# Reordering the opening of a one-core Trainium2 kernel: where decays are clipped, when they are stored, and how the first gates arrive

## The chip, the core and the metric

The kernel runs on one core of a Trainium2 chip. The core has five engines, each with its own stream of instructions: TensorE (PE: matrix products, written to PSUM), VectorE (DVE), ScalarE (ACT), GpSimd (POOL) and SyncE (SP, which here only issues transfers, or DMAs, between DRAM and on-chip memory). ScalarE and GpSimd issue a few transfers too. An engine takes its instructions in order, and one that waits for a semaphore holds everything behind it. The metric is the device time of one execution, in microseconds (us), as the median of several runs. Less is better.

## What is computed

Two blocks in a row. The first is a state-space recurrence (Mamba-2 style) over 4 sequences of 768 tokens with 8 heads of width 32 and state size 16; the second mixes 4 experts, each a two-layer network of width 1024, over the resulting 3072 tokens of width 256.

```python
log_a = np.log(np.clip(a, 1e-06, 1.0))
for c in range(nc):
    ...
    cum = np.cumsum(la, axis=-1)
    L = np.exp(cum[:, :, :, None] - cum[:, :, None, :]) * causal
    CB = np.einsum('bhin,bhjn->bhij', Cc, Bc)
    y_intra = np.einsum('bhij,bhjd->bhid', CB * L, xc)
    y_inter = np.einsum('bhin,bhnd->bhid', Cc, state) * decay_to_i[:, :, :, None]
    y[:, :, sl] = y_intra + y_inter
    state = decay_full[:, :, None, None] * state + np.sum(Bx, axis=2)
...
p = domain_probs / (domain_probs.sum(-1, keepdims=True) + 1e-09)
for e in range(E):
    h = np.maximum(x @ w1[e], 0.0)
    out += p[:, e:e + 1] * (h @ w2[e])
```

The decays `a` are clipped to [1e-6, 1]; running products of them weigh the scores C·B; the weighted scores times x are the outputs y. The probabilities p, one for each token and expert, are the gates of the second block.

## The kernel before

Tokens are cut into 24 chunks of 128; four chunks, one of each sequence, make a block of 512 tokens, so there are 6 blocks. The two-layer networks run over a block in 8 steps (expert by half of its width), 48 steps in all; steps n = 2 to 47 form a loop, and each uses a scheme with seven products instead of eight, whose weight sums GpSimd makes once (`sum_w1`, `sum_w2`) and stores for later blocks. Recurrence work for the next block is woven into the loop. Steps 0 and 1 of the first block use plain products (`plain_first`, `plain_gated`, `plain_second`).

The order of all instructions is written out by hand: each engine's queue is the program's order, and semaphores are set from what tiles are written and read. A transfer issued by SP or ScalarE also waits until the one eight before it in the program's order has landed, since eight semaphores are used in turn.

One chunk goes through these helpers:

- `clip_first(engine, c)`, for chunks 0 to 2 only: clips the raw decays, already laid out for the products, into a_q (two operations at L279 and a small memset at L287).
- `spread(c, homes)`: 16 passes at L362 copy the decays over partitions into PSUM (tiles named a).
- `decays(c)`: VectorE's scans at L395 make the running products LT; GpSimd's L400 makes the part of MT that feeds the state. From chunk 3 on the scans read a tile ab that `load_decays` (L147, SP's queue) brings from the DRAM copy acut_d.
- `masks(c)`: two ScalarE operations (L411) that prepare B.
- `scores(cs, homes)`: TensorE's L429, tile g.
- `masked(cs, rs)`: VectorE's L441 multiplies g by LT into MT. `aside(c, 3)` does one of the four head groups by ScalarE (copy, L447) and GpSimd (L448).
- `outputs(cs, homes)`: TensorE's L488 gives y; ScalarE copies it to yT (L501) and the state part to A (L508, L509, L511).

The decays of all chunks are clipped and cut into a_cut by GpSimd (L302 to L307) and stored by ScalarE's queue with `store_decays` (L314 to acut_d, L311 to ac_d). The gates pr are normalized by GpSimd and VectorE (L294 to L300), turned round by TensorE (L323, tile pp), copied (L326) and stored to p_d (L327, SP's queue). Each later expert's gates come back from p_d with `load_gate` (L347), spread over all partitions. Those of the first block's first expert are made without that transfer: `spread_gate` spreads them by four products with columns of the identity (L337, tile gp), and `keep_gate` copies the result (L343).

`turn(n, w)` (L776) issues n products of width w x 128 whose result nobody reads. In what follows they are called unread products. They multiply the tile `ones`, which VectorE sets at L230.

The opening, in order (main part):

```python
turn(1); turn(1, 2); spread(0, banks); turn(1, 3)
masks(0); scores([0], homes); turn(1, 2)
decays(0); aside(0, 3); store_decays(0)
masks(1); spread(1, banks); masked([0], (2, 0, 1)); clip_first(nc.gpsimd, 2)
load_rows(2); load_w1(1); store_decays(1)
turn_gates(ps_att, "att"); turn(1, 2); outputs([0], ATT)
scores([1], ...); decays(1); aside(1, 3)
load_x(2); load_rows(3); load_decays(3); load_w2(0); load_x(3)
spread(2, ...); spread_gate((0, 1), ps_att, "att"); masked([1], (0, 1, 2)); masks(2)
outputs([1], ...); spread_gate((2, 3)); keep_gate(); sum_w1(0, 0)
load_w2(1); load_w1(2); load_w2(2); decays(2); plain_first(0, 1, (0,)); ...
```

Of the kernel before, what the change touches and what calls it, by code (L numbers as in the profile page):

```python
# [8 lines left out]
FP32 = mybir.dt.float32  # L9
# [3 lines left out]
P = 128  # L13
# [4 lines left out]
def kernel(  # L18
# [40 lines left out]
    nc = tc.nc  # L59

    NCH, _, W = xbc.shape
    E, DM, F = w1.shape
# [4 lines left out]
    CPB = BLK // P  # L67
    NBLK = NCH // CPB
    T = NCH * P
# [8 lines left out]
    def real(c):  # L78

        return c % CPB * NBLK + c // CPB  # L80
# [7 lines left out]
    att = ctx.enter_context(tc.tile_pool(name="att", bufs=2))  # L88
    ffn = ctx.enter_context(tc.tile_pool(name="ffn", bufs=2))
    ps_att = ctx.enter_context(tc.tile_pool(name="ps_att", bufs=2, space=bass.MemoryType.PSUM))  # L90
    ps_f = ctx.enter_context(tc.tile_pool(name="ps_f", bufs=1, space=bass.MemoryType.PSUM))
    ps_s = ctx.enter_context(tc.tile_pool(name="ps_s", bufs=1, space=bass.MemoryType.PSUM))
# [5 lines left out]
    p_d = tc.dram_tile([T // P, E, P], FP32, name="p_d")  # L98
# [7 lines left out]
    HALF = P // 2  # L106
# [5 lines left out]
    def turned_round(c):  # L112


        return c >= CPB and c % 2 == 1

    def load_rows(c):

        xb = load.tile([P, OCT + P], FP32, tag="xb", name="xb", bufs=4)
        src = xbc[real(c)][:, WX:]  # L120
        if turned_round(c):
            nc.sync.dma_start(out=xb[:HALF, OBT:], in_=src[HALF:])
            nc.sync.dma_start(out=xb[HALF:, OBT:], in_=src[:HALF])
        else:
            nc.sync.dma_start(out=xb[:, OBT:], in_=src)
        st.setdefault(c, {})["xb"] = xb
# [17 lines left out]
    def load_decays(c):  # L144
        ab = load.tile([P, NQ, TRI], FP32, tag="ab", name="ab")
        for t in range(NT):
            nc.sync.dma_start(  # L147
                out=ab[HALF * t:HALF * t + HALF].rearrange("p q s -> p (q s)"),
                in_=acut_d[t, real(c)].rearrange("q s -> (q s)").partition_broadcast(HALF))
        st.setdefault(c, {})["ab"] = ab  # L150
# [73 lines left out]
    a_sb = const.tile([NCH * NH // 2, 2, P], FP32, name="a_sb")  # L224
# [4 lines left out]
    ones = const.tile([P, P], FP32, name="ones")  # L229
# [3 lines left out]
    for queue, c in ((nc.sync, slice(0, 1)), (nc.scalar, slice(1, SPREAD))):  # L233
        queue.dma_start(
            out=a_raw.rearrange("(q r) c t s -> q r c (t s)", q=NQ)[:, 0, c],
            in_=a.rearrange("(i k) (q t) s -> k q i (t s)", k=NBLK, t=NT)[0][:, c])
# [4 lines left out]
        out=a_sb, in_=a.rearrange("c h s -> (c h) s").rearrange("(p r) s -> p r s", r=2))  # L241
# [6 lines left out]
    ident = const.tile([P, P], FP32, name="ident")  # L248
# [19 lines left out]
    for q in range(NQ):  # L268
        rows = slice(32 * q, 32 * q + 32)
# [8 lines left out]
    def clip(engine, v, top=1.0, out=None):  # L278
        engine.tensor_scalar(out=v if out is None else out, in0=v, scalar1=1e-6, scalar2=top,  # L279
                             op0=ALU.max, op1=ALU.min)  # L280

    def clip_first(engine, c):


        clip(engine, a_raw[:, c], own, a_q[:, c, :, :P])
        clip(engine, a_raw[:, c, :, HALF:], own, a_q[:, c, :, P:])
        engine.memset(a_q[:, c, :, 0:P + 1:P], 0.0)  # L287

    clip_first(nc.vector, 0)
    clip_first(nc.vector, 1)  # L290


    pairs = const.tile([P, T // P, 2], FP32, name="pairs")
# [5 lines left out]
    nc.vector.reciprocal(total_p, total_p)  # L299
    nc.gpsimd.tensor_mul(pr, pr, total_p.to_broadcast([P, T // P, E]))  # L300

    clip(nc.gpsimd, a_sb)  # L302

    a_cut = const.tile([NCH * NQ, NT, TRI], FP32, name="a_cut")
    nc.gpsimd.tensor_copy(a_cut[:, :, :P], a_sb)
    nc.gpsimd.tensor_copy(a_cut[:, :, P:], a_sb[:, :, HALF:])
    nc.gpsimd.memset(a_cut[:, :, 0:P + 1:P], 0.0)  # L307

    def store_decays(kind):
        if kind:  # L310
            nc.scalar.dma_start(  # L311
                out=ac_d.rearrange("c h s -> (c h) s").rearrange("(p r) s -> p r s", r=2), in_=a_sb)
        else:
            nc.scalar.dma_start(  # L314
                out=acut_d.rearrange("t c q s -> (c q) t s"), in_=a_cut)

    gate = {}

    def turn_gates(pool, tag):

        rows = T // P * E
        pp = pool.tile([rows, P], FP32, tag=tag, name="pp")
        nc.tensor.transpose(pp, pr.rearrange("p i e -> p (i e)"), ident)  # L323
        p_sb = const.tile([rows, P], FP32, name="p_sb")
        gate["rows"] = p_sb
        nc.scalar.copy(out=p_sb, in_=pp)  # L326
        nc.sync.dma_start(out=p_d.rearrange("i e s -> (i e) s"), in_=p_sb)  # L327

    def spread_gate(parts, pool=None, tag=None):

        p_sb = gate["rows"]
        if 0 in parts:
            gate["all"] = pool.tile([P, CPB, P], FP32, tag=tag, name="gp")
        g = gate["all"]
        for i in parts:
            r = real(i) * E
            nc.tensor.matmul(  # L337
                out=g[:, i], lhsT=ident[:T // P * E, r:r + 1].to_broadcast([T // P * E, P]),
                rhs=p_sb, start=(i == 0), stop=True, skip_group_check=True)

    def keep_gate():
        gate[0, 0] = ffn.tile([P, CPB, P], FP32, tag="gate", name="gate", bufs=3)
        nc.scalar.copy(out=gate[0, 0], in_=gate["all"])  # L343

    def load_gate(k, e):
        g = gate[k, e] = ffn.tile([P, CPB, P], FP32, tag="gate", name="gate", bufs=3)
        nc.sync.dma_start(out=g, in_=p_d.rearrange(  # L347
            "(i k) e s -> k e i s", k=NBLK)[k, e].partition_broadcast(P))
# [4 lines left out]
    def spread(c, homes):  # L353


        s = st[c]
        s["a"] = []
        for q, (pool, tag) in enumerate(homes):
            k = slice(32 * q, 32 * q + 32)
            b = pool.tile([P, TRI], FP32, tag=tag, name="a")  # L360
            for t in range(NT):
                nc.tensor.matmul(  # L362
                    out=b[HALF * t:HALF * t + HALF], lhsT=ones[k, :HALF], rhs=a_q[k, c, t],
                    start=True, stop=True, tile_position=(32 * q, HALF * t), skip_group_check=True)
            s["a"].append(b)
# [39 lines left out]
    def masks(c):  # L405


        s = st[c]
        m = s["btm"] = att.tile([HN, 2, NT, HALF], FP32, tag="btm", name="btm")
        for t in range(NT):  # L410
            nc.scalar.mul(  # L411
                m[:, :, t], s["xb"][:, OBT:OBT + P].rearrange("p (h j) -> p h j", h=2),
                tmask[:, t:t + 1])

    def scores(cs, homes):

        for c in cs:
            st[c]["g"] = {}
        for r, (pool, tag) in enumerate(homes):
            g = pool.tile([P, len(cs), 3, HALF], FP32, tag=tag, name="g")  # L420
            for j, c in enumerate(cs):
                st[c]["g"][r ^ 2 * turned_round(c)] = g[:, j]
        for j, c in enumerate(cs):
            s = st[c]
            for h in range(2):
                for r in range(NQ):
                    k = slice(32 * r, 32 * r + 32)
                    g = s["g"][r ^ 2 * turned_round(c)].rearrange("p h i -> p (h i)")
                    nc.tensor.matmul(  # L429
                        out=g[:, P * h:P + HALF * h],  # L430
                        lhsT=s["btm"][k, h].rearrange("p t j -> p (t j)"),
                        rhs=s["xb"][k, OCT + HALF * h:OCT + P],
                        start=(j == 0 and h == 0), stop=True, tile_position=(32 * r, 0),
                        skip_group_check=True)
# [334 lines left out]
    ATT = ((ps_att, "att"), (ps_att, "att"))  # L769
    banks = ((ps_f, "X"), (ps_f, "Y"), (ps_s, "acc2"), (ps_s, "acc3"))  # L770

    def turn(n, w=4):

        for _ in range(n):
            t = ps_att.tile([P, w, P], FP32, tag="att", name="t")
            nc.tensor.matmul(out=t, lhsT=ones, rhs=ones.unsqueeze(1).to_broadcast([P, w, P]),  # L776
                             start=True, stop=True)

    turn(1)
    turn(1, 2)  # L780
    spread(0, banks)
    turn(1, 3)
    masks(0)
    scores([0], homes)
    turn(1, 2)
    decays(0)
    aside(0, 3)
    store_decays(0)
    masks(1)
    spread(1, banks)  # L790
    masked([0], (2, 0, 1))
    clip_first(nc.gpsimd, 2)
    load_rows(2)
    load_w1(1)
    store_decays(1)
    turn_gates(ps_att, "att")
    turn(1, 2)
    outputs([0], ATT)
    scores([1], ((ps_s, "acc0"), (ps_s, "acc1"), (ps_att, "att"), (ps_f, "X")))
    decays(1)  # L800
    aside(1, 3)
    load_x(2)
    load_rows(3)
    load_decays(3)
    load_w2(0)
    load_x(3)
    spread(2, ((ps_s, "acc2"), (ps_s, "acc3"), (ps_f, "Y"), (ps_s, "acc0")))
    spread_gate((0, 1), ps_att, "att")
    masked([1], (0, 1, 2))
    masks(2)  # L810
    outputs([1], (ATT[0], (ps_s, "acc1")))
    spread_gate((2, 3))
    keep_gate()
    sum_w1(0, 0)
    load_w2(1)
    load_w1(2)
# [53 lines left out]
    for n in range(PLAIN, NS):  # L870
        k, r = divmod(n, SPB)
# [8 lines left out]
        e = r // JJ  # L880
# [138 lines left out]
```

## Time and profile before

| | |
|---|---|
| median of 9 runs | 642.23 us (639.24 to 645.97) |
| profiled execution: its time | 642.23 us |
| profiled execution: span from first to last instruction | 640.4 us |
| TensorE busy | 634.4 us, 99% |
| VectorE busy | 470.4 us, 73% |
| ScalarE busy | 124.0 us, 19% |
| GpSimd busy | 109.0 us, 17% |
| transfers | 122.16 MB, mean 191 GB/s |

The profile is of one execution. Its page gives busy times, the chain of work that ended last (followed back from the last instruction), and groups of instructions with what ended the idle time before them. A timeline lists instructions in order of time: start, length, engine and line, output and inputs, how many. The line numbers are those of the kernel before. "Landing" of a transfer is the time from its issue to its last completion.

Because the share of TensorE is 99%, the page as a whole says little of the change, which lies in the first 27 us or so. GpSimd, at 17% of the span, is busy for most of the first 60 us: its work is nearly all in the opening.

### The profile page before, as it was taken

Reading aid. Unit: us, or ns where it says so; the run is one execution under the profiler, and the core shown is the slowest. Engines: PE = TensorE matmul, PEld = TensorE weight load, DVE = VectorE, ACT = ScalarE, POOL = GpSimd, SP = SyncE. Lnnn points to the kernel's source line nnn. Section 1 sums busy time; section 2 is a strip of 40 time slices with the busy share of each in tenths; the row PEclk is TensorE's granted clock in tenths of the full one; section 3 lists DMA queues with packets and bytes.
Section 4 is the critical chain, followed back from the end, with each engine's and each line's share of the span. In section 5 each row is a group of like instructions: output and inputs, shape, how many; then the busy total and the mean of one; then the engine's idle time right before and its main releaser. Section 6 shows DMA issues by size and latency. Waiting matters only on the chain.

```text
span 640.4 us, 10765 instructions
## 1 busy us (share of the span) xinstructions
PE 634.4 (99%) x4089; PEld 545.0 (85%) x4089; DVE 470.4 (73%) x814; ACT 124.0 (19%) x314; POOL 109.0 (17%) x169
## 2 busy tenths in 40 slices
PE   8999999999999999999999999999999999999997
PEld 4888888888888888888888888888888888888886
DVE  6667989787776878777778768678876676756555
ACT  3211121212121221122121212122111212111110
POOL 6785738020000002000002000000200000100001
PEclk9999999999999999999999999999999999999999
DMA  6899788397646468546729754647786754157001
GB/s 195 238 338 336 230 212 339 115 262 224 204 118 198 181 196 270 171 161 195 249 79 291 252 169 118 208 169 207 246 206 204 253 175 133 60 142 248 3 1 34
DMA packets 104136, 122.16 MB, mean 191 GB/s; under 512 B 30440, under 2 KB 89108, under 8 KB 104084
## 3 DMA queue, kind: packets, MB, share of 16 engines
q1 hardware_dynamic: 101032, 111.60, 56.9%
q0 software_dynamic: 2432, 9.50, 3.8%
q8 instruction: 32, 0.52, 0.3%
q10 hardware_dynamic: 620, 0.37, 0.2%
q14 instruction: 20, 0.16, 0.1%
HBM read 108.56 MB, written 12.88 MB: 190 GB/s over the span
## 4 chain that ended last, share of the span: by engine, by line
PE 99%; DVE 1%; issue 0%; ACT 0%
PE acc L654 44%; PE X L569 25%; PE Y L569 19%; PE acc L635 2%; PE g L429 2%; PE y L488 2%; PE X L618 1%; PE Y L618 1%; PE y L466 1%; PE t L776 1%; PE a L362 0%; PE gp L337 0%; DVE qmask L270 0%; DVE a_q L279 0%; PE turned L701 0%
## 5 line engine op out<-in xcount | busy, mean ns | idle before, releaser
L581 DVE TENSOR_TENSOR z<-Y,snap 128x512 f32<-128x512 f32 x138 | 94.9, 688 | 137.8 <-PE Y L569 69.3
L654 PE MATMUL acc<-hT,wt 128*128 128x256 f32 x736 | 181.0, 379 | 0.0
L576 ACT COPY snap<-X 128x512 f32<-128x512 f32 x138 | 80.8, 586 | 425.1 <-PE X L569 423.1
L654 PEld LDWEIGHTS acc<-hT,wt 128*128 128x128 f32 x736 | 139.8, 190 | 19.0
L654 PE MATMUL acc<-h,wt 128*128 128x256 f32 x552 | 143.6, 383 | 0.0
L569 PE MATMUL X<-yS,wt 128*128 128x256 f32 x552 | 141.7, 379 | 0.0
L569 PEld LDWEIGHTS X<-yS,wt 128*128 128x128 f32 x552 | 104.8, 190 | 14.5 <-issue 0.3
L654 PEld LDWEIGHTS acc<-h,wt 128*128 128x128 f32 x552 | 103.1, 190 | 15.0
L591 DVE SCALAR_TENSOR_TENSOR h<-z,gate 128x512 f32<-128x512 f32 x138 | 99.2, 719 | 3.5 <-PE acc L635 0.4
L569 PE MATMUL Y<-yT,wt 128*128 128x256 f32 x368 | 94.4, 379 | 0.0
L569 PEld LDWEIGHTS Y<-yT,wt 128*128 128x128 f32 x368 | 68.8, 190 | 10.6
L598 DVE TENSOR_TENSOR hT<-h,hT 128x512 f32<-128x512 f32 x92 | 66.5, 723 | 1.8
L598 DVE TENSOR_TENSOR hT<-h,h 128x512 f32<-128x512 f32 x92 | 62.2, 717 | 1.1
L569 PE MATMUL X<-yT,wt 128*128 128x256 f32 x184 | 47.3, 379 | 0.0
L569 PE MATMUL Y<-yS,wt 128*128 128x256 f32 x184 | 47.2, 379 | 0.0
L400 POOL TENSOR_TENSOR MT<-xb,LT 128x128 f32<-128x128 f32 x20 | 9.5, 473 | 187.7 <-PE Y L569 98.3
L395 DVE TENSOR_TENSOR_SCAN LT<-ab,own_i 128x384 f32<-128x384 f32 x42 | 40.8, 982 | 0.0
L591 DVE SCALAR_TENSOR_TENSOR h<-X,gate 128x512 f32<-128x512 f32 x50 | 34.5, 689 | 8.5 <-PE X L569 4.5
L569 PEld LDWEIGHTS X<-yT,wt 128*128 128x128 f32 x184 | 34.9, 190 | 4.9 <-issue 0.2
L569 PEld LDWEIGHTS Y<-yS,wt 128*128 128x128 f32 x184 | 35.0, 190 | 4.7
L381 POOL TENSOR_TENSOR cts<-xb,dec 128x128 f32<-128x128 f32 x20 | 8.9, 465 | 156.0 <-DVE dec L378 91.1
L441 DVE TENSOR_TENSOR MT<-g,LT 128x192 f32<-128x192 f32 x94 | 26.0, 348 | 2.2 <-PE g L429 2.2
(103 smaller groups left out, 345.4 us busy)
## 6 DMA issues: line engine op xcount, KB each, us to landing
wt<-in_w_dram SPq DMA_DIRECT2D x112, 256.0 KB, 6.1
wt<-w_d SPq DMA_DIRECT2D x40, 640.0 KB, 7.1
wt<-w_d SPq DMA_DIRECT2D x40, 512.0 KB, 8.3
ab<-acut_d SPq DMA_DIRECT2D x42, 192.0 KB, 3.2
gate<-p_d SPq DMA_DIRECT2D x23, 256.0 KB, 6.7
w_d<-wt POOLq DMA_DIRECT2D x8, 640.0 KB, 6.4
wt<-in_w_dram SPq DMA_DIRECT2D x40, 128.0 KB, 9.0
xb<-in_xbc_dram SPq DMA_DIRECT2D x38, 128.0 KB, 3.1
```

Source lines behind the costliest of these rows:

```text
L395: nc.vector.tensor_tensor_scan(out=LT[:, i * w:i * w + w], data0=s["a"][i], data1=own_i.rearrange("p q h i -> p (q h i)")[:, :w], initial=0.0,
L429: nc.tensor.matmul(out=g[:, P * h:P + HALF * h], lhsT=s["btm"][k, h].rearrange("p t j -> p (t j)"), rhs=s["xb"][k, OCT + HALF * h:OCT + P] ...
L441: nc.vector.tensor_mul(s["MT"][:, q, :, :HALF], s["g"][q], s["LT"][:, q])
L488: nc.tensor.matmul(out=y, lhsT=halves(c)[rows, h, OX[t] + 32 * q:OX[t] + 32 * q + 32], rhs=m, start=(k == 0 and h == 0), stop=(h == 1), ti ...
L569: nc.tensor.matmul(out=f[bank][:, j], lhsT=wt1[n][:, w, j * P:j * P + P], rhs=rhs, start=(i in (1, 2, 5) and j == 0), stop=(j == JJ - 1), ...
L576: nc.scalar.copy(out=s, in_=first[n]["X"])
L581: nc.vector.tensor_add(z, first[n]["Y"], first[n][i])
L591: nc.vector.scalar_tensor_tensor(out=h, in0=first[n][src], scalar=0.0, in1=g.unsqueeze(1).to_broadcast([P, JJ, HB]), op0=ALU.max, op1=ALU. ...
L598: nc.vector.tensor_sub(h[o], h[x], h[y])
L618: nc.tensor.matmul(out=f[bank][:, j], lhsT=wt1[n][:, w, j * P:j * P + P], rhs=yT[k][:, i, cols], start=(i == 0 and j == 0), stop=(i == 1), ...
L635: nc.tensor.matmul(out=acc[k, u][:, half], lhsT=w2_op(n, w)[:, j], rhs=hid[n][f"{i + 1}{b}"][:, j], start=(begins and i == 0 and j == 0), ...
L654: nc.tensor.matmul(out=acc[k, u][:, half], lhsT=w2_op(n, w)[:, j], rhs=rhs[:, j], start=(begins and j == 0), stop=(n % SPB == SPB - 1 and ...
```

## The change

It does the following:

- Chunk 1's `clip_first` moves from VectorE to GpSimd, after the gates' normalization.
- The clip and cut of all decays (`cut_decays`) move in GpSimd's order from before chunk 0's state part to after chunk 2's `clip_first`.
- Both `store_decays` and `load_decays(3)` move to after the outputs of chunk 1. In ScalarE's queue the stores thus stand behind chunk 1's copies, and in SP's queue the load of chunk 3's decays stands behind `load_w2(0)` and `load_x(3)`.
- `turn_gates` moves up to before the scores of chunk 0, and its store to p_d goes out on ScalarE's queue instead of SP's.
- `spread_gate` and `keep_gate` are gone; `load_gate(0, 0)` brings the first expert's gates from p_d, on SP's queue behind `load_w1(1)`.
- The unread products multiply a constant of the program (1.0, one column, repeated) which is set before the engines are released. There are two of width 512 and one of width 256, instead of one of 512, one of 384 and three of 256.
- Chunk 1's outputs use the same PSUM tag for both halves.

```diff
     clip_first(nc.vector, 0)
-    clip_first(nc.vector, 1)
...
-    clip(nc.gpsimd, a_sb)
+    clip_first(nc.gpsimd, 1)
...
-    nc.gpsimd.tensor_copy(a_cut[:, :, :P], a_sb)
-    nc.gpsimd.tensor_copy(a_cut[:, :, P:], a_sb[:, :, HALF:])
-    nc.gpsimd.memset(a_cut[:, :, 0:P + 1:P], 0.0)
+    def cut_decays():
+        clip(nc.gpsimd, a_sb)
+        nc.gpsimd.tensor_copy(a_cut[:, :, :P], a_sb)
+        nc.gpsimd.tensor_copy(a_cut[:, :, P:], a_sb[:, :, HALF:])
+        nc.gpsimd.memset(a_cut[:, :, 0:P + 1:P], 0.0)
...
-        gate["rows"] = p_sb
         nc.scalar.copy(out=p_sb, in_=pp)
-        nc.sync.dma_start(out=p_d.rearrange("i e s -> (i e) s"), in_=p_sb)
+        nc.scalar.dma_start(out=p_d.rearrange("i e s -> (i e) s"), in_=p_sb)
...
-            nc.tensor.matmul(out=t, lhsT=ones, rhs=ones.unsqueeze(1).to_broadcast([P, w, P]),
-                             start=True, stop=True)
-    turn(1)
+            one = nc.const_aps.tensor(1.0, [P, 1])
+            nc.tensor.matmul(
+                out=t, lhsT=one.to_broadcast([P, P]),
+                rhs=one.unsqueeze(1).to_broadcast([P, w, P]), start=True, stop=True)
+    turn(2)
+    spread(0, banks)
+    masks(0)
+    turn_gates(ps_att, "att")
     turn(1, 2)
-    spread(0, banks)
-    turn(1, 3)
-    masks(0)
     scores([0], homes)
-    turn(1, 2)
     decays(0)
     aside(0, 3)
-    store_decays(0)
     masks(1)
     spread(1, banks)
     masked([0], (2, 0, 1))
     clip_first(nc.gpsimd, 2)
+    cut_decays()
     load_rows(2)
     load_w1(1)
-    store_decays(1)
-    turn_gates(ps_att, "att")
-    turn(1, 2)
+    load_gate(0, 0)
     outputs([0], ATT)
     scores([1], ((ps_s, "acc0"), (ps_s, "acc1"), (ps_att, "att"), (ps_f, "X")))
     decays(1)
     aside(1, 3)
     load_x(2)
     load_rows(3)
-    load_decays(3)
     load_w2(0)
     load_x(3)
     spread(2, ((ps_s, "acc2"), (ps_s, "acc3"), (ps_f, "Y"), (ps_s, "acc0")))
-    spread_gate((0, 1), ps_att, "att")
     masked([1], (0, 1, 2))
     masks(2)
-    outputs([1], (ATT[0], (ps_s, "acc1")))
-    spread_gate((2, 3))
-    keep_gate()
+    outputs([1], ATT)
+    store_decays(0)
+    store_decays(1)
+    load_decays(3)
     sum_w1(0, 0)
```

## The prediction

> **What bounds the kernel now.** I read the shares of the chain that ended last first, then that chain in order of time, then each engine's timeline over the first 30 us. The page's shares:
>
> ```profile
> PE 99%; DVE 1%; issue 0%; ACT 0%
> ```
>
> TensorE is the bound. In the chain in order of time (start us, us, what) it is left only in the opening:
>
> ```profile
> 4.48 0.10 DVE a_q L279
> 4.57 0.04 issue
> 4.62 0.94 PE a L362 x16
> ...
> 8.26 0.37 DVE MT L441
> 8.62 0.04 issue
> 8.67 1.22 PE t L776 x2
> ...
> 16.22 0.64 PE gp L337 x4
> 16.86 1.73 PE X L618 x8
> ...
> 26.57 0.54 PE y L488 x32
> 27.11 3.65 PE acc L635 x16
> ```
>
> See three things. TensorE's first needed products (decays of chunk 0, tile a) wait for VectorE's clip at 4.57. From 8.67 on TensorE has one gap over 0.1 us (0.18 at 22.27) until the last transposes. So a microsecond is won or lost only by what precedes the long stretch of weight products. The checkpoint I use is the end of chunk 3's outputs, y(3), at 27.11: behind it both kernels issue the same products. The timelines of the opening (start us, us busy, engine, line; the bracket is idle time and what ended it):
>
> ```profile
> 5.88 1.07 POOL L279 TENSOR_SCALAR a_sb<-a_sb 96x256 f32<-96x256 f32 x1
> 7.70 0.10 POOL L307 MEMSET a_cut<- 96x4 f32 x1
> 8.41 0.36 ACTq L314 DMA_DIRECT2D acut_d<-a_cut  x1
> 8.74 0.59 POOL L448 TENSOR_TENSOR MT<-gs,LT 128x192 f32<-128x192 f32 x1 [0.50 <-ACT gs L447]
> 9.45 1.93 POOL L279 TENSOR_SCALAR a_q<-a_raw,own 128x256 f32<-128x256 f32 x2
> 11.43 0.11 POOL L287 MEMSET a_q<- 128x4 f32 x1
> 11.93 1.10 PE L488 MATMUL y<-MT,xb 64*32 64x144 f32 x32
> 13.87 1.12 SPq L147 DMA_DIRECT2D ab<-acut_d  x2
> 15.61 0.61 PE L488 MATMUL y<-MT,xb 64*32 64x144 f32 x32
> 21.77 1.80 DVE L395 TENSOR_TENSOR_SCAN LT<-ab,own_i 128x384 f32<-128x384 f32 x2
> 23.48 1.13 DVE L441 TENSOR_TENSOR MT<-g,LT 128x192 f32<-128x192 f32 x4
> ```
>
> The same 32 output products take 1.10 at 11.93 and 0.61 at 15.61: TensorE runs at half its later rate until about 13, though the profile's granted clock reads 1.00 in every slice. And chunk 3's decays leave (acut_d) at 8.41, come back (ab) from 13.87, and are scanned only at 21.77, with time to spare.
>
> **The change, step by step.**
>
> **1. Start.** The unread products no longer wait for VectorE's ones (0.84 to 1.00), so they start near 0.74, when the engines are released, not 1.06. Four passes of 512 columns at the record spacings of before (1.02 for the first, 0.85 for the next) end at 0.74 + 1.02 + 3 x 0.85 = 4.3. Tile a(0) still waits for VectorE at 4.57. Worth nothing; its cover is that clip.
>
> **2. VectorE loses chunk 1's clip** (0.39 net). The reciprocal moves from 5.06 to about 4.57, so GpSimd's pr (0.35) ends at 5.30 instead of 5.79 and the transpose pp can follow a(0) at 5.5. Between a(0) and the scores, 384 columns of unread product become pp plus 256: pp 0.25, product 0.9, scores from 6.65 (7.07 before), done 7.8 (8.23). VectorE's scans still end at 7.47. Gain 0.4.
>
> **3. Two unread products of 256 columns go**, with pp from its old place. At 8.67 to 9.82 and 10.69 to 11.93 they cost 1.15 + 1.24. Chunk 1's a now follows the scores at 7.8, if GpSimd has its clip by then: GpSimd takes it at 5.38, for 1.93 + 0.16 by the row of 9.45, done 7.47. It is hidden, by 0.3. Then a(1) ends at 8.67, and y(0) waits for GpSimd's product of head group 3 (scores out by ScalarE 7.93 to 8.25, then 0.59): 8.92. y(0) thus starts 3.0 us earlier than 11.93.
>
> **4. GpSimd becomes the wait.** Behind that product stand chunk 2's clip (2.10: 9.03 to 11.13), all decays' clip and cut (5.88 to 7.80 before, 1.93: done 13.1), and only then chunk 1's state part (0.41) and head group 3 (0.59): done 14.2, against 15.25 before. VectorE's share of chunk 1 is ready at 12.0. So y(1) stalls 2.2 us on TensorE and ends at 14.8, against 16.24. This returns 1.6 of the 3.0 us. If chunk 2's clip slowed beside VectorE, each 0.1 is 0.1 here; the a_sb clip ran beside VectorE's scans at its usual pace, so I add nothing.
>
> **5. The gate's products go** (two at 0.64 by the chain) and ScalarE's 0.59 copy. The second 0.64 hid ScalarE's yT copies, so 0.3 appears: X starts at 15.15, against 16.86: 1.7 earlier. In their place the gates go out on ScalarE's queue at about 7.3 and come back as one 256 KB transfer on SP's queue. The store of before took 2.8 us from issue to landing (trace: 11.46 to 14.24), acut_d took 4.3 on ScalarE's queue: back-load issued at 10.2 to 11.7. Its 512 packets of 34 ns (trace, at 29 to 35 us) are 1.1 us of 16 engines, behind weights that landed at 13.8: landed by 15 to 16. The next gate took 6.2 from issue, which would be 16.4 to 17.9. VectorE asks for it at X's end, 16.9, with the masked scores of chunk 2 queued behind; they have 1 us of slack. Bounds 0 to nothing visible, since step 6 waits longer anyway. Value 0.
>
> **6. The decays' round trip moves behind y(1).** ScalarE issues acut_d only after y(1)'s copies, near 15.2 (6.8 later than 8.41; at worst 16.0 behind the four state copies, which end 1.15 after the first). Landing takes 2.8 (p_d's row) to 4.3 (acut_d's own); I take 3.7, since the queue is loaded but less than then: 18.9. SP, which now has the ab loads behind x(3), waits there. Two issues, then landing 3.2 after the second (the page's median for ab) to 4.4 (trace: 14.39 to 18.82); I take 3.8 as the queue has run nearly empty: 18.9 + 0.65 + 3.8 = 23.35. Then by the rows of 21.77 and 23.48 scan and masked scores take 2.84, and y(3) ends 0.55 after: 26.7. Without this wait y(3) would end at 15.15 + 10.25 (its distance from X before) = 25.4. So 1.3 of the 1.7 us is given back. Ends: 18.0 + 0.65 + 3.2 + 3.4 = 25.3, no wait at all; 20.3 + 0.65 + 4.4 + 3.4 = 28.75.
>
> **7. Behind SP's wait** stand the transfers of w2(1), w1(2), w2(2), chunk 4 and the next gate: about 3 us later (w2(1) 21.3, was 18.24). GpSimd's sums of w2 start 25.7 instead of 24.07. First uses: TensorE takes w1(2) at 40.96, its sums at 44.4 (GpSimd had them at 32.0), the gate at 43.7 (landed 35.3). At least 8 us of cover: 0. If it were gone, at most those 3 us.
>
> **Sum.** y(3) ends at 26.7 instead of 27.11: -0.4. Profiled span 640.4 becomes 640.0; the profiled execution took 642.23, which is also the median, so 1.8 lies around the span: **641.8 us**.
>
> [...]
>
> **Rivals.**
>
> *A, the opening's gain survives.* The round trip is short: acut_d as fast as p_d, ab at the median. For it: the stores no longer compete with the first weights. Then y(3) ends at 25.3 to 25.5, and if TensorE also reaches full rate before y(0) (0.49 less there), 24.9: -1.7 to -2.2, 640.0 to 640.5. Against it: both ends must be the short ones.
>
> *B, slower: TensorE stays at half rate.* Before, it reached full rate 4.4 us after its last gap (8.67 to 13.1). The changed order leaves gaps at 8.7 and 10.0 (0.2 to 0.3 each) and 2.2 us at 12.0; the stretch without gaps begins at about 15.2. If every gap counts as much as the one before 8.67 did, full rate comes 4.4 us after that, near 19.6; y(1) is 0.5 later (1.10 against 0.61), X starts at 15.65, and the 3.95 us until 19.6 do only 2.0 us of work: y(3) ends at 25.4 + 0.5 + 2.0 = 27.9, +0.8, 643.0; with twice that time to full rate another 2.2 is lost, 645.2. It decides over step 6 as soon as the half rate lasts past 18. Against it: from 0.74 to 8.67 TensorE has only one gap of 0.3, so it may be warm by 8.
>
> *C, slower: the round trip at its loaded end* (4.3 and 4.4, ScalarE's issue at 16.0): y(3) ends at 28.75, +1.6: 643.9. Each microsecond beyond a landing of 23.8 costs one.
>
> *D, GpSimd's clip is not hidden in step 3*: a(1) late by what it exceeds; absorbed by step 4, so no change from the forecast.
>
> **Chances.** Forecast 0.45 (with D), A 0.20, B 0.20, C 0.12, something else 0.03. About 0.5%, 3.2 us, is what a measurement of this kernel can tell from no change (the nine runs spread from 639.24 to 645.97). No case reaches it by itself; the scatter of a median, about 1 us, and a mis-sized term do. Faster by over 0.5% (under 639.0): a third of A, some of the rest, 0.10. Slower (over 645.4): a quarter of B, a third of C, the rest: 0.13. Within: 0.77. The range reaches from A less 1 us to the late end of B: 639.0 to 645.0.
>
> **What would show it.** y(0) near 8.9 and y(1) cut in two by a wait on GpSimd's MT L448; X near 15.2; ScalarE's store of acut_d near 15.2 and VectorE's scan of ab near 23.4 with TensorE idle before y(3) by 1 to 1.5 us. The first y group at 0.6 instead of 1.1 means the clock came early; X at over 3 us for its 8 passes means B. I am wrong if the scan starts before 22 (A) or after 25 (C), if VectorE waits for the gate at 17 to 19, or if gaps appear on TensorE after 30 us.

## The result, and the profile after

| | before | after |
|---|---|---|
| median | 642.27 us (54 runs, 639.24 to 646.29) | 647.95 us (17 runs, 644.5 to 650.14) |
| ratio to before | | 1.0082, 95% interval 1.0063 to 1.0101 |
| profiled execution | 642.23 us, span 640.4 | 645.14 us, span 643.4 |

The change costs 5.7 us, where 0.4 less was forecast. The range ended at 645.0. The profiled execution of after took 2.8 us less than the median; a second profile, at the median, is shown further down.

The shares of the chain that ended last, after:

```profile
PE 95%; DMA 2%; SPq 1%; POOL 1%; issue 0%; DVE 0%; ACT 0%; POOLq 0%
```

TensorE no longer has 99%: transfers, their issues and GpSimd hold 4 of the points. The chain in order of time (start us, us, what) says where:

```profile
7.45 3.44 DMA xb<-in_xbc_dram
...
15.05 6.39 DMA acut_d<-a_cut
21.45 0.02 issue
...
24.90 3.62 DMA wt<-in_w_dram
28.52 0.02 issue
28.54 1.29 PE y L474 x25
29.83 3.65 PE acc L621 x16
```

The checkpoint, the end of y(3), is at 29.83 against 27.11. From there on after stays 2.72 us behind before: the first products and their results h are the same 2.7 us late at 38 us, at 64 us and at 540 us. So the loss is made before 30 us. The long step is the store of the decays, 6.39 us. (The chain names the weights `wt` last. They landed at 28.52; by the timeline what y(3) reads was ready at 28.48, so at most 0.04 us of its wait is theirs.) The timeline of after (start us, us busy, engine, line; in brackets the idle time before it and what ended it):

```profile
7.27 0.35 ACTq L329 DMA_DIRECT2D p_d<-p_sb  x1
8.23 1.16 PE L474 MATMUL y<-MT,xb 64*32 64x144 f32 x32 [0.18 <-DVE MT L427]
10.91 1.06 POOL L279 TENSOR_SCALAR a_sb<-a_sb 96x256 f32<-96x256 f32 x1
11.43 0.39 SPq L333 DMA_DIRECT2D gate<-p_d  x1
13.31 1.62 PE L474 MATMUL y<-MT,xb 64*32 64x144 f32 x32 [1.84 <-POOL MT L386]
15.05 0.33 ACTq L317 DMA_DIRECT2D acut_d<-a_cut  x1
15.16 3.78 PE L604 MATMUL X<-yT,wt 128*128 128x256 f32 x8 [0.23 <-ACT yT L487]
18.98 0.69 DVE L577 SCALAR_TENSOR_TENSOR h<-X,gate 128x512 f32<-128x512 f32 x1 [5.54 <-PE X L604]
21.51 1.12 SPq L147 DMA_DIRECT2D ab<-acut_d  x2
26.13 1.81 DVE L381 TENSOR_TENSOR_SCAN LT<-ab,own_i 128x384 f32<-128x384 f32 x2 [3.65 <-DMA ab<-acut_d]
28.07 0.41 POOL L386 TENSOR_TENSOR MT<-xb,LT 128x128 f32<-128x128 f32 x1 [5.50 <-DMA wt<-in_w_dram]
28.54 1.29 PE L474 MATMUL y<-MT,xb 64*32 64x144 f32 x32 [1.34 <-DMA wt<-in_w_dram]
```

Read it from the end. y(3) starts 0.06 us after GpSimd's state part (28.07 + 0.41), which follows VectorE's scan (26.13 + 1.81 = 27.94), which waited 3.65 us for the decays to come back. SP could ask for them only at 21.51, when the store had landed.

Two things are new. The stretch from 12 to 20 us, with the busy time of each engine, the mean granted clock, the share of the transfer engines and GB/s at the end of a line:

```profile
12.00:16.00 4.00, 2.46 (x34) 1.72 (x35) 1.44 (x4) 1.57 (x8) 3.73 (x8) 0.58 0.50 93
16.00:20.00 4.00, 4.00 (x24) 2.84 (x24) 0.84 (x2) 0.01 (x1) 0.22 (x2) 0.56 1.02 236
```

First, the transfers move 93 GB/s from 12 to 16 us (before: 250): the gates' transfer is running then. Second, the granted clock is 0.58 and 0.56. The records behind these means give full rate from 5.85 us, half from 12.68, full again from 19.51. That is why X takes 3.78 instead of 1.89 us.

### The profile page after: what moved, and what is told of

Its sections match the earlier page's. It is cut to its first block, busy times and chain, and to the rows that moved or that the text cites. A ratio compares the mean times of both kernels' runs of the same rounds, so it can differ in the third digit from the quotient of the medians.

```text
span 643.4 us, 10747 instructions
## 1 busy us (share of the span) xinstructions
PE 634.0 (99%) x4077; PEld 544.4 (85%) x4077; DVE 471.1 (73%) x811; ACT 123.4 (19%) x313; POOL 112.8 (18%) x172
## 2 busy tenths in 40 slices
DMA packets 104663, 122.41 MB, mean 190 GB/s; under 512 B 30456, under 2 KB 89636, under 8 KB 104612
## 4 chain that ended last, share of the span: by engine, by line
PE 95%; DMA 2%; SPq 1%; POOL 1%; issue 0%; DVE 0%; ACT 0%; POOLq 0%
PE acc L640 44%; PE X L555 25%; PE Y L555 19%; PE acc L621 2%; PE y L474 2%; PE g L415 2%; PE y L452 1%; DMA acut_d<-a_cut 1%; DMA wt<-in_w_dram 1%; PE Y L604 1%; PE X L604 1%; DMA xb<-in_xbc_dram 1%; SPq L136 0%; SPq L187 0%; SPq L175 0%
## 5 line engine op out<-in xcount | busy, mean ns | idle before, releaser
L584 DVE TENSOR_TENSOR hT<-h,h 128x512 f32<-128x512 f32 x92 | 64.0, 736 | 1.1
```

The costliest lines, as they stand in the source:

```text
L584: nc.vector.tensor_sub(h[o], h[x], h[y])
```

## Experiments

The loss was put to three theories. **G**: the gates' transfer takes some 7 us and holds back what is beside and behind it. **W**: TensorE's wait for GpSimd at y(1) lets the clock fall to half. **R**: the late round trip of the decays is long by itself. Each median is compared with runs of before made beside it on the same chip (their medians are 642.2 to 642.4); ratios are to these, and intervals are 95%. Edits are shown in short, without the bodies of helpers that come back.

### Undoing parts of the change

**Gates by products again**, the rest as after:

```diff
-    load_gate(0, 0)
+    spread_gate((0, 1), ps_att, "att")
...
-    outputs([1], ATT)
+    outputs([1], (ATT[0], (ps_s, "acc1")))
+    spread_gate((2, 3))
+    keep_gate()
```

> The changed kernel, but the first expert's gates are made by products as before (no gate transfer among the first loads); decays still stored late. Three theories. G (the gate transfer, 6.9 us from issue to landing, holds back the loads and stores around it): acut_d lands 3.5 to 4.3 us after its issue instead of 6.4, chunk 3's scan starts near 23.5, y(3) ends near 26.7, median 642 to 643.5. W (the wait of y(1) for GpSimd lets TensorE's clock fall to half): that wait is still there, 1.5 to 2 us, X takes about 3.5 us, median 645 to 648. R (the late round trip of the decays is long in itself): scan after 25, y(3) ends after 29, median 645 or more.

645.76 us, ratio 1.0054 (1.0030 to 1.0078). The decays' store landed in 1.9 us (19.48 to 21.42) and y(3) had no wait, as G says. But the run brought a fault of its own: with one transfer fewer, the eight semaphores fell differently, and ScalarE's store of the gates had to wait for another load. In the trace its semaphore was last used by the first load of x(1), issued at 6.14 and landed at 10.53; in after it was that of the second load of x(0), landed at 7.19. (The semaphores go round in an order that is not quite that of the source: in after the store takes its turn behind `load_w1(1)`, here behind `load_rows(3)`.) ScalarE's copy stood behind it:

```profile
10.61 0.39 ACTq L330 DMA_DIRECT2D p_d<-p_sb  x1
11.04 0.32 ACT L450 COPY gs<-g 128x192 f32<-128x192 f32 x1 [5.15 <-DMA xb<-in_xbc_dram]
```

y(0) then waited 3.6 us, and the clock fell from 10.73 to 20.97. So 645.76 is no price for the gates' transfer.

**Decays' clip, stores and load at their old places**, gates by the transfer:

```diff
+    clip_first(nc.vector, 1)
...
-    clip_first(nc.gpsimd, 1)
...
+    cut_decays(); store_decays(0)
...
+    store_decays(1)
...
+    load_decays(3)
...
-    store_decays(0); store_decays(1); load_decays(3)
```

> The changed kernel, but chunk 1's clip, the clip and cut of all decays, their stores and chunk 3's load as before; the gate still comes by a transfer. G: the loads behind the gate are still late, VectorE waits for the gate or TensorE for chunk 2's x until 18 to 19, y(3) ends near 27.5 to 28.5, median 643 to 645. W: y(1) no longer waits for GpSimd, the clock stays full, median 640 to 642. R: the scan of chunk 3 does not wait, median 640 to 642.

643.85 us, 1.0025 (1.0006 to 1.0045): 4.1 us less than after. In its profile no wait of TensorE above 0.3 us is left in the opening, yet X took 3.78 us: full rate came only at 19.92, though the unread products start as in after.

**Both undone**, only the start as after, which is the two edits above together:

```diff
+    clip_first(nc.vector, 1)
...
+    store_decays(0)
...
-    load_gate(0, 0)
+    store_decays(1)
+    load_decays(3)
+    spread_gate((0, 1), ps_att, "att")
...
+    spread_gate((2, 3))
+    keep_gate()
```

> Both undone: gates by products and decays as before; what stays of the change are the unread products from the program's constants, fewer of them, and the gates' transposition moved up. All theories: faster than before, since y(0) starts some 2 to 3 us earlier and nothing waits for GpSimd or the gate: median 639 to 641, y(3) ends at 24.5 to 25.5. If it is not faster than before, what limits is none of the three.

646.06 us, 1.0058 (1.0035 to 1.0081). A miss for every theory, and the fault of the first run again: ScalarE issued the gates' store at 11.05 instead of 7.27, and behind it

```profile
12.48 1.07 PE L493 MATMUL y<-MT,xb 64*32 64x144 f32 x26 [3.73 <-POOL MT L453]
```

**Filling the wait at y(1)** with two unread products of width 512:

```diff
     masks(2)
+    turn(2)
     outputs([1], ATT)
```

> The changed kernel with two more unread products of width 512 on TensorE ahead of chunk 1's outputs, where it sits idle for GpSimd. W: the clock stays full through the opening and the median falls by 3 us or more, to 645 or below. G and R: the decays' round trip still sets y(3), which ends at 29.5 to 30 as in the changed kernel's profile, though X now takes 1.9 instead of 3.8 us; the median falls no lower than the profiled execution of the changed kernel, 645.

648.89 us (6 runs), 1.0103 (1.0064 to 1.0143). The wait before y(1) is gone, but the clock still fell, for 3.4 us from 11.52. The decays' store now had to wait for the gates' landing (18.76), on ScalarE, and y(3) waited longer than ever:

```profile
18.84 0.33 ACTq L317 DMA_DIRECT2D acut_d<-a_cut  x1
28.55 1.81 DVE L381 TENSOR_TENSOR_SCAN LT<-ab,own_i 128x384 f32<-128x384 f32 x2 [7.28 <-DMA ab<-acut_d]
30.96 1.66 PE L474 MATMUL y<-MT,xb 64*32 64x144 f32 x32 [4.75 <-POOL MT L386]
```

**All decays' clip one step later on GpSimd**, behind head group 3 of chunk 1, so that y(1) has nothing to wait for:

```diff
-    cut_decays()
...
     aside(1, 3)
+    cut_decays()
```

> The changed kernel with the clip and cut of all decays moved behind chunk 1's products on GpSimd, so that TensorE no longer waits 1.8 us for y(1). W: the clock does not fall to half in the opening (or 7 us less of it), X takes 1.9 us, median 643 to 645. G and R: the store is still issued near 15 and the gate is as slow, the scan of chunk 3 starts at 25.5 to 26.5, y(3) ends at 29 to 30 and its wait of 3 us or more lets the clock fall later: median 646 to 648.5.

646.19 us (7 runs), 1.0077 (1.0049 to 1.0106): 1.8 less than after. y(1) came at 11.73 without the wait, X at 13.58. The clock fell all the same (11.67 to 18.50), X took 3.78, and y(3) waited 2.08 for the decays. Together with the run before it, this takes W down as the cause: without that wait the clock still fell and most of the loss stayed.

### Doing one part alone

**Gate by the transfer**, the rest as before (p_d stored by SP):

```diff
+    load_gate(0, 0)
...
-    spread_gate((0, 1), ps_att, "att")
...
-    spread_gate((2, 3))
-    keep_gate()
```

> The kernel before with one part of the change: the first expert's gates by a transfer instead of products. G (the gate transfer is slow, about 7 us, and what is queued behind it is late): issued near 14.3, after p_d has landed, landed near 20 to 21; VectorE, which asked for it near 18, waits 2 to 3 us, and the loads behind it are late by 3 us: median 644 to 647. R or W alone: the decays are stored early and TensorE does not wait for GpSimd, so no loss: 641 to 642.5.

645.48 us, 1.0048 (1.0023 to 1.0073): +3.2. Here VectorE does wait for the gates, TensorE with it, and again at 38 us:

```profile
14.09 0.38 SPq L347 DMA_DIRECT2D gate<-p_d  x1
19.65 0.69 DVE L591 SCALAR_TENSOR_TENSOR h<-X,gate 128x512 f32<-128x512 f32 x1 [2.90 <-DMA gate<-p_d]
21.45 0.71 PE L488 MATMUL y<-MT,xb 64*32 64x144 f32 x32 [0.66 <-DVE MT L441]
37.99 1.99 PE L618 MATMUL Y<-yT,wt 128*128 128x256 f32 x8 [1.60 <-DVE h L591]
```

**Late clip, stores and load of the decays**, the rest as before:

```diff
-    clip(nc.gpsimd, a_sb)
...
     clip_first(nc.gpsimd, 2)
+    cut_decays()
...
-    store_decays(0)
...
-    load_decays(3)
...
     keep_gate()
+    store_decays(0)
+    store_decays(1)
+    load_decays(3)
```

> The kernel before with one part of the change: all decays clipped and cut after chunk 2's clip, stored after chunk 1's outputs, chunk 3's decays loaded after x(3). R (the late round trip): acut_d issued near 16.5, landed 19.5 to 21, scan of chunk 3 at 24 to 25.5 instead of 21.8, y(3) ends at 27.5 to 29: median 643 to 644.5. G: without the gate transfer acut_d lands within 3.5 us and little is lost: 641.5 to 643. W: GpSimd's head group 3 of chunk 1 is done before TensorE asks, the clock does not fall, no loss: 641.5 to 642.5.

645.20 us, 1.0045 (1.0024 to 1.0066): +2.9, more than any of the three theories had here. R is not the reason: the store landed in 2.0 us and TensorE did not wait for y(3). What its profile shows is a late clock: X takes 2.75 us from 18.75, and full rate begins at 20.48.

**Unread products from the program's constants**, the rest as before:

```diff
-            nc.tensor.matmul(out=t, lhsT=ones, ...)
+            one = nc.const_aps.tensor(1.0, [P, 1])
+            nc.tensor.matmul(out=t, lhsT=one.to_broadcast([P, P]), ...)
-    turn(1)
-    turn(1, 2)
+    turn(2)
     spread(0, banks)
```

> The kernel before with one part of the change: the unread products take the program's constants and the first two are both of width 512, so TensorE starts at 0.74 and has no gap until 4.6. All theories: TensorE's clock may rise earlier, at 4 to 10 us instead of 10 to 16; if it stays up, y(0) to X take 1 to 2 us less, median 640 to 642; if the gap before 8.67 lets it fall again, median 642 to 645.

**639.90 us** (12 runs, 639.14 to 641.13), 0.9969 (0.9949 to 0.9990): 2.4 faster than before, and faster than both kernels. Full rate begins at 6.06 and stays; X takes 1.89 us at 14.07. The edit does two things that were not tried apart: it takes the constant, and the second product is 512 instead of 256 columns wide. TensorE starts at 0.78 instead of 1.06, and the gap of 0.64 us ahead of a(0) is gone.

**Everything but the gates' transfer**: after with the gates by products, and their store on SP's queue, where it does not hold up ScalarE:

```diff
-        nc.scalar.dma_start(out=p_d.rearrange("i e s -> (i e) s"), in_=p_sb)
+    def store_gates():
+        nc.sync.dma_start(out=p_d.rearrange("i e s -> (i e) s"), in_=gate["rows"])
...
-    load_gate(0, 0)
+    store_gates()
+    spread_gate((0, 1), ps_att, "att")
...
+    spread_gate((2, 3))
+    keep_gate()
```

> The changed kernel without its gate transfer: the first expert's gates are spread by products again, the gates' store goes out by SyncE; decays late, constants and shorter unread products as changed. G (the gate transfer lengthens the decays' store and load beside costing time itself): acut_d lands 2 to 3 us after its issue instead of 6.4, y(3) waits under 0.5 us for the decays, time 642.0 to 644.0. W (the wait at y(1) for GpSimd lets the clock fall, whatever the transfer): clock half rate for 6.8 us from 11 to 13 on, time 643.5 to 645.5. R (the late round trip is long by itself): acut_d over 4 us, y(3) waits over 1 us, 646.5 to 648.5.

642.81 us, ratio 1.0 (0.9973 to 1.0026): 5.1 less than after, the whole loss but half a microsecond. The timeline:

```profile
13.19 1.53 PE L493 MATMUL y<-MT,xb 64*32 64x144 f32 x32 [1.21 <-POOL MT L405]
15.97 0.34 ACTq L317 DMA_DIRECT2D acut_d<-a_cut  x1
18.71 1.12 SPq L147 DMA_DIRECT2D ab<-acut_d  x2
23.11 1.81 DVE L400 TENSOR_TENSOR_SCAN LT<-ab,own_i 128x384 f32<-128x384 f32 x2 [1.76 <-DMA ab<-acut_d]
25.99 0.80 PE L493 MATMUL y<-MT,xb 64*32 64x144 f32 x32
```

TensorE still waits at y(1) for 1.2 us, but the decays' store, issued 0.9 us later than in after, lands in 2.7 us, and y(3) does not wait. It is near the forecast's picture: the scan starts at 23.1 (23.35 forecast) and y(3) ends at 26.8 (26.7), though without the idle time before it that the forecast had, as the clock held X up (2.43 us, half rate from 13.32 to 16.73).

### What makes the transfer slow

The products that came back also fill part of the wait at y(1), so two more runs kept them out. **A quarter of the gates' transfer**:

```diff
+    early = ffn.tile([P, CPB, P], FP32, tag="gate", name="gate", bufs=3)
+    nc.scalar.copy(out=early, in_=nc.const_aps.tensor(1.0, [P, 1])...)
...
     def load_gate(k, e):
+        if (k, e) == (0, 0):
+            gate[k, e] = early
+            nc.sync.dma_start(out=early[:, 0], in_=p_d.rearrange(
+                "(i k) e s -> k e i s", k=NBLK)[k, e, 0].partition_broadcast(P))
+            return
```

> The changed kernel with a quarter of the gate transfer: only the first of the four chunks of 128 gates is loaded (64 KB in 128 rows of 512 bytes), the other three are left at 1.0, set by ScalarE near the start, so those rows of the output are not weighed by their gate. Every other instruction as in the changed kernel, no products of the gates. G (the transfer's load on the queues carries the loss, over the decays' store and load): gate lands 2.5 to 4 us after its issue, the decays' store within 4, y(3) waits under 0.5 us, time 642.5 to 645. F (what the kernel without the transfer gained came from the gates' products, which fill TensorE's wait at y(1)): y(3) waits little, but the time stays at 646.5 to 648.5.

643.05 us, 1.0010 (0.9990 to 1.0031). The wait at y(1) is 1.48 us and X takes 3.17, yet 4.9 us are gone; F falls, G stands. The gates landed in 3.2 us, the store in 3.4. The fall of the clock at y(1) did not make the difference: it came here too, with half rate for 6.83 us from 10.59, as long as in the first profile of after.

**The same 256 KB in pieces of 2 KB**: the gates lie in DRAM by block, expert and chunk, so a gate is one row:

```diff
-    p_d = tc.dram_tile([T // P, E, P], FP32, name="p_d")
+    p_d = tc.dram_tile([NBLK, E, CPB, P], FP32, name="p_d")
...
-    nc.gpsimd.tensor_mul(pr, pr, total_p.to_broadcast([P, T // P, E]))
+    nc.gpsimd.tensor_mul(pk.rearrange("p k e i -> p i k e"), ...)
...
-        nc.sync.dma_start(out=g, in_=p_d.rearrange(
-            "(i k) e s -> k e i s", k=NBLK)[k, e].partition_broadcast(P))
+        nc.sync.dma_start(out=g, in_=p_d[k, e].partition_broadcast(P))
```

> The changed kernel with the gates kept in DRAM by block, expert and chunk, so that one gate is 2 KB in a row: the same 256 KB go to 128 partitions as 128 pieces of 2 KB instead of 512 of 512 bytes. P (the number of small packets sets the transfer's time): gate lands 2.5 to 4.5 us after its issue instead of 6.9, decays' store under 5, time 643 to 646. B (its bytes, or that all partitions read the same 2 KB, set it): gate lands 6 to 7 us after issue, decays' store over 5.5, time 647 to 649.

643.44 us, 1.0019 (1.0003 to 1.0034): 4.5 less than after, with every byte moved, and again with half rate for 6.83 us (from 11.32). P stands. The packets of all transfers, and the time from issue to landing of the 24 gates' transfers, in after:

```profile
DMA packets 104663, 122.41 MB, mean 190 GB/s; under 512 B 30456, under 2 KB 89636, under 8 KB 104612
DMA to landing us min/median/max: 6.1/6.6/7.3
```

and with rows of 2 KB:

```profile
DMA packets 95447, 122.41 MB, mean 191 GB/s; under 512 B 30456, under 2 KB 77348, under 8 KB 95396
DMA to landing us min/median/max: 3.8/3.9/5.7
```

There are 9216 packets fewer (24 times 384) for the same 122.41 MB, and the landing is 2.7 us sooner. y(3) waits 0.58 us. In the trace's packet records the 512 packets of the first gate start over 5.2 us (12.5 to 17.7), the 128 packets of 2 KB over 2.4 us (12.3 to 14.7). The decays' store, beside it, lands later the longer the gates' transfer takes. Only the first row has the gates' products; where two numbers stand, the second is from the second profile further down:

| first gate's transfer | gate, issue to landing | decays' store, issue to landing | median |
|---|---|---|---|
| none | | 2.7 us | 642.81 |
| 128 x 512 B | 3.2 us | 3.4 us | 643.05 |
| 128 x 2 KB | 4.2 us | 4.6 us | 643.44 |
| 512 x 512 B | 6.9, 7.0 us | 6.4, 7.3 us | 647.95 |

For the same 128 packets, four times the bytes add 1.0 us to the gates' landing; for the same bytes, four times the packets add 2.7.

No single price of a packet fits the three: 5.2 us over 512 packets are 10.2 ns each, the 128 packets of the quarter took 1.7 us by the trace, 13.5 ns each, and the 128 of 2 KB took 2.4 us, about 19 ns each.

**2 KB rows in the fastest version** (the constants alone, with the same edit):

> The fastest kernel so far (the one before with its unread products from the program's constants, 639.9) with the gates in DRAM as in the run beside it, 2 KB in a row. Later gates arrive sooner there by P, but all are hidden: 639.5 to 640.3 by either theory; under 639.5 if the gates' traffic still holds something up there.

639.87 us, 0.9961 (0.9942 to 0.9979): the same as without (639.90). Later gates are hidden, so their packets cost nothing there.

### Second profiles

> The changed kernel once more, for a second profile: its median is 647.95 and the first profiled execution took only 645.14, with half rate for one stretch of 6.8 us. If the clock makes the scatter: an execution near 648 shows half rate for two stretches (10 to 14 us in all), the second begun by the wait before y(3); an execution near 645 shows one.

647.86 us, span 646.1. Its clock records show half rate from 13.01 to 19.84 and again from 30.08 to 33.49. The second profile of after:

```profile
11.43 0.39 SPq L333 DMA_DIRECT2D gate<-p_d  x1
15.35 0.33 ACTq L317 DMA_DIRECT2D acut_d<-a_cut  x1
22.69 2.15 SPq L147 DMA_DIRECT2D ab<-acut_d  x2
27.56 1.81 DVE L381 TENSOR_TENSOR_SCAN LT<-ab,own_i 128x384 f32<-128x384 f32 x2 [4.76 <-DMA ab<-acut_d]
29.97 1.66 PE L474 MATMUL y<-MT,xb 64*32 64x144 f32 x32 [2.45 <-POOL MT L386]
```

The store takes 7.3 us here, y(3) waits 2.45, and at 30.08 the clock falls a second time, as it does in the two other runs with a wait of over 2 us there (4.75 and 2.08); after waits of 1.34 and 0.58 it did not. y(3) takes 1.66 us, and the products behind it run at half rate until 33.49. At 38 us this execution is 5.45 us behind before, which is the loss of the medians. So these two profiles differ by one transfer and by the clock after it. That this makes the whole scatter of after (644.5 to 650.14) rests on two executions.

> The kernel before once more, for a second profile. If the scatter of its runs (about 639.5, 642.3 and 645.3) is set by when full rate begins: an execution near 639.5 has full rate from 6 to 10 us, one near 642.3 from 13, one near 645.3 from 19 to 20. If something else makes the scatter, the times do not order with the start of full rate.

639.27 us, full rate from 4.53. This profile of before:

```profile
12.60 0.61 PE L488 MATMUL y<-MT,xb 64*32 64x144 f32 x32
13.70 1.89 PE L618 MATMUL X<-yT,wt 128*128 128x256 f32 x8
```

> As the run before it: an execution near 639.5 has full rate from 6 to 10 us, one near 642.3 from 13, one near 645.3 from 19 to 20; otherwise the times do not order with it.

645.76 us, full rate only from 21.87. This profile of before:

```profile
16.79 1.00 PE L488 MATMUL y<-MT,xb 64*32 64x144 f32 x32
18.73 3.45 PE L618 MATMUL X<-yT,wt 128*128 128x256 f32 x8
```

The first profile of before, with 642.23, had full rate from 13.13. The three times order with it, though 4.53 and 21.87 lie outside the stretches expected for them (6 to 10 and 19 to 20). Of the 103 runs of before made beside these experiments 22 lie at 639.1 to 640.5, 55 at 641.4 to 642.7 and 26 at 644.9 to 646.3, with none between; of the 54 in the result's table three do (640.75, 640.76 and 641.13). The executions at 642.23 and 645.76 have the same waits of TensorE, and its products start at the same times to 0.01 us until 12.96; what differs from there is the clock.

## Why the prediction was wrong

Most of the opening came as worked out. What failed is the price of two transfers, and that two rivals came together.

1. *Start, "worth nothing".* The products did start at 0.78 (0.74 forecast), and a(0) did wait for the clip. But the worth is 2.4 us by the run with the constants alone (and a wider second product). I priced the start by what waits for what; its effect is on the clock. Both profiles with the constants and the old order behind them have full rate by 6.1 us (4.60 and 6.06), where before's three begin at 4.5, 13.1 and 21.9. The start is no guarantee: with the decays at their old places it was the same, and full rate came at 19.92.
2. *VectorE's clip, 0.4.* pp came at 5.49 (5.5 forecast), the scores at 6.32 (6.65). The unread product between them took 0.66 us (0.9 forecast), as full rate had begun at 5.85; the profile of before has half rate there.
3. *Unread products go.* y(0) at 8.23 (8.92 forecast); a(1) waited 0.36 for GpSimd's clip, as in rival D, but still came at 7.46, ahead of the 7.8 forecast, since the scores were done sooner.
4. *GpSimd becomes the wait.* Right: stall of 1.84 at y(1) (2.2 forecast). That its end came as forecast, 14.9 (14.8), is in part luck: GpSimd was done at 13.80 (14.2), but y(1) ran on until 14.93 at half rate, where the forecast had full rate.
5. *Gates.* X at 15.16 (15.15 forecast). **This step failed in "landed by 15 to 16" and "value 0".** I counted 512 packets at 34 ns over 16 engines, 1.1 us, and gave the observed 6.2 us of a later gate only as a second reading, landed by 16.4 to 17.9. It landed at 18.28, 6.85 us after its issue, and I counted as its cost only a wait of VectorE, not what it does to the store of step 6. The view of the gates' tile in the profile of before, with all 23 later gates, already had it:

```profile
DMA to landing us min/median/max: 6.2/6.7/6.9
```

   23 transfers in all kinds of traffic that take 6.2 to 6.9 us point to the transfer itself, and the run with 2 KB rows shows it: 3.9 us for the same bytes. In after itself VectorE does not wait for the gates, since X ends only at 18.94; the cost is paid by the transfer beside them.
6. *The decays' round trip.* Issue at 15.05 (15.2 forecast). **"Landing takes 2.8 to 4.3" failed: 6.4, and 7.3 at the median.** The queue I took to be less loaded held the gates. Without them it takes 2.7 us, the short end. The rest of the step held: from the landing to the scan 4.7 us (4.45 forecast), and y(3) ends 3.7 after the scan's start (3.35). From 18.9 forecast to 21.45 for the landing are 2.55 of the 3.1 us by which y(3) ended late (29.83, 26.7 forecast).
7. *Behind SP's wait, 0.* Right for after: the lag stays at 2.72 from 38 us on. The run with the gate alone shows that the cover is thinner than the 8 us I gave: there TensorE waits 1.6 us at 38, behind VectorE's scan of the next chunk's decays. The second half of their load was issued at 29.64 and landed at 35.72; the step had not listed that scan among the first uses.

The rivals: **C** (loaded round trip) was the mechanism, beyond the end that I gave it: its sign, a scan after 25, came at 26.13. **B** had full rate at 19.6, and it came at 19.5, but by coincidence: B had the clock not rise before, while it rose at 5.85 and fell again at 12.68. In the first profile B costs nothing beside C: by the timeline, X's lost 1.9 us lie under the wait for the decays. In the median execution the wait grows until the clock falls a second time, and that adds: y(3) takes 1.1 us more, and the products after it lose about half of 1.9 us. I had them as alternatives and summed neither with the other.

By the runs, added up in this order, the 5.7 us are about: the start, -2.4; the late decays without the gates' transfer +2.9 (645.20 against 642.31, and 642.81 against 639.90, though this second pair differs also in the unread products, the place of `turn_gates` and the engine of chunk 1's clip); the gates' transfer +5.1 on top of both, though it costs only 3.2 alone. The parts are not independent. Alone it delays VectorE and, at 38 us, TensorE; with the late decays it also delays the store that sets y(3), as the table of the four transfers shows.

**What stays open.** What lets the clock fall or keeps it from rising is not settled. The order of instructions alone does not set it: the three profiles of before have one order and three starts of full rate (4.53, 13.13 and 21.87). In the run with the filled wait it fell at 11.52, after a stretch of 6.83 us at full rate in which TensorE was idle for only 1.4 us in all (gaps over 0.1 us: 0.74, 0.26, 0.13, 0.28), and in the run with late decays alone TensorE worked without a gap from 8.69 on and yet ran at half rate until 20.48. Part of that work are products on 32 rows (tiles a and g, `32*64` and `32*128` in the trace); what they do to the clock was not tried by itself. That +2.9 us of the late decays is the clock rests on that one profile. On TensorE it agrees to 0.03 us, until its full rate begins, with the execution of before that took 645.76, which has no late decays; so why all 12 of its runs lie at 644.16 to 646.58 is not shown. And no run was made to move a rise or a fall of the clock by itself.

## What to carry to other kernels

Price a transfer by its own row in the trace, issue to landing, over all its instances: a time that stays high in all kinds of traffic (here 6.2 to 6.9 us over 23 gates) points to the transfer, not its neighbours, and a run with the same bytes in fewer packets can settle it (here 3.9 us with a quarter of the packets). Count packets as well as bytes, and add what else is in flight when a store on the critical path is issued. And on a kernel bound by TensorE, look at the clock records of several executions before a change to the opening is judged: here one start without gaps was worth 2.4 us, more than any reordering tried behind it.

## Not expected of the hardware

- The time of before lies, but for three runs of 157, in three clusters 3 us apart, and three profiles tie them to the start of TensorE's full rate (4.5, 13.1, 21.9 us). With the start from constants the spread of the runs shrinks from 7 us to 2 us.
- The records hold, once full rate has been reached, stretches at one rate in the opening of 3.41 us (half rate, 30.08 to 33.49 in the second profile of after), of 6.83 (the first profile of after: full 5.85 to 12.68, half 12.68 to 19.51) and of 10.24 (half rate, 10.73 to 20.97 in the first run with the gates by products; full rate, 19.84 to 30.08 in the second profile of after): one, two and three times 3.413, half of the 6.827 of the first profile of after.
- 256 KB spread from 2 KB of DRAM to 128 partitions take 6.6 us (median) in packets of 512 B and 3.9 in packets of 2 KB. From 12 to 16 us, beside the first of them, all transfers together move 93 GB/s with the small packets and 203 with the 2 KB rows.
- A transfer on ScalarE's queue that waits for its semaphore stops ScalarE's own work: 3.6 and 3.7 us on TensorE in the two runs where the eight semaphores, going round in turn, gave the gates' store that of a load still under way.
